# Gated linear attention and an MLP-Mixer on one core: held loads, crossbar transposes and reordered token mixing

## The chip, the cores and the metric

The kernel runs on one core of one Trainium2 chip. The metric is the device time of one execution, in microseconds (us). Most executions of a kernel agree to within a few tenths of a per cent up to about one per cent. An execution that takes over 1.5% longer than the fastest one of the same kernel is called slow and is left out of the comparisons; those that remain are called fast.

Five engines matter here. TensorE (PE in the profile, PEld for its weight loads) does the matrix products. VectorE (DVE) and ScalarE (ACT) do elementwise work and empty PSUM, the memory that TensorE writes its products to. GpSimd (POOL) issues most loads, and SyncE (SP) issues the rest of the DMA transfers. In this kernel every engine works through its own queue in the order of the program, so an instruction that waits also holds up what stands behind it.

## The reference

There are two stages: a gated linear attention whose state is updated token by token, and an MLP-Mixer on its result. B=4, H=8, S=768, D=48; the mixer sees x of shape 4 x 768 x 384.

```python
f = 1.0 / (1.0 + np.exp(-f_logit))
for t in range(S):
    state = f[:, :, t, :, None] * state + np.einsum('bhd,bhe->bhde', k[:, :, t], v[:, :, t])
    y[:, :, t] = np.einsum('bhd,bhde->bhe', q[:, :, t], state)
# ... x = y with the heads side by side: 4 x 768 x 384
h = np.maximum(x.transpose(0, 2, 1) @ w_tok1, 0.0) @ w_tok2     # token mixing, d_tok = 256
u = x + h.transpose(0, 2, 1)
h2 = np.maximum(u @ w_ch1, 0.0) @ w_ch2                         # channel mixing, d_ch = 1536
return u + h2
```

## The kernel before

The attention is done in chunks of 128 tokens, six to a batch, in this way:

- **Gates.** ScalarE turns the forget logits into logarithms of f. They are split into a bf16 high part `Lhi` and a low part `Llo`; the low part is a subtraction.
- **Decayed q and k.** A product with a triangular matrix sums the logarithms over the chunk. Their exponentials `G` and `Gi` scale q and k to `qh` and `kh`.
- **Turning.** `qh` and `kh` have tokens on the partitions. For the scores they are needed with the head dimension there, so TensorE multiplies them by an identity, four products for the eight heads, and ScalarE or VectorE copies the result out of PSUM to `qT` and `kT`.
- **Scores, mask, readout.** The scores are masked (`Am`), and the readout adds the part inside the chunk to the part that comes from the state. The state is copied to a block-diagonal bf16 tile, `state_bd`, for this.

The mixer follows for each batch: token mixing (`tok1`, relu, `tok2`), the sum u, its bf16 copy, three transposing products for each 128 tokens, and the two channel products (`ch1`, `ch2`). In the profile `w_ch_68` is the weight of the first channel product, `w_ch_69` that of the second, and `w_tok_67` that of the second token-mixing product.

```python
if b == 0:                                    # forget logits of batch 0, on SyncE's queue
    for c in range(NCH):
        n = add({"SP": 0.05}, lambda e, c=c: nc.sync.dma_start(out=f_sb[i][:, :, c, :], in_=src[:, :, c, :]),
                key, [])
        made["f", b, c] = add({"Q": 1.1}, None, key + 0.06 * c, [n])
# ... gates: the low half
o = add({"POOL": 0.85 * n, "DVE": 0.4 * n + 0.08} if b > 1 else {"DVE": 0.4 * n + 0.08},
        lambda e: on(e).tensor_tensor(lo, fb, hi, ALU.subtract), key, [g, h])
# ... attention, chunk c of batch b; j = c % 2, p2 = the chunk two before
def turn(name, src, n):
    def fn(e):
        t[name] = p = bank("att", name)
        a = blk(src)
        for hp in range(HP):
            nc.tensor.matmul(p[:, hp * 128:(hp + 1) * 128], lhsT=a[:, hp, :], rhs=ident,
                             start=True, stop=True)
    return fn
tq = made["Tq", b, c] = add({"PE": 0.25}, turn("pq", qh[j], 0), key, [qh_, made.get(("y", *p2))], bank="att")
tk = made["Tk", b, c] = add({"PE": 0.25}, turn("pk", kh[j], 0), key, [kh_, made.get(("A", *p2))], bank="att")
flat = {"ACT": 0.5, "DVE": 0.6}
cq = add(flat, lambda e: copy(e, qT[j], t["pq"].rearrange("p (a t) -> p a t", a=4)),
         key, [made.get(("y", *p2))], frees=tq)
# ... the same for kT
def diag(e):
    copy(e, state_bd[j][0:D, :, 0:D], state[j][0:D])
    copy(e, state_bd[j][64:64 + D, :, D:2 * D], state[j][64:64 + D])
made["bd", b, c] = add({"DVE": 0.5, "ACT": 0.55}, diag, key + 0.02, [s_, made.get(("y", *p2))])
# ... the readout takes state_bd[1 - j], so the one of chunk c - 1
# ... mixing: u, turned on TensorE
def utr(e, tt=tt, t=t):
    t["p"] = bank("mix", "pm")
    for m in range(3):
        nc.tensor.matmul(t["p"][:, m * 128:(m + 1) * 128], lhsT=u_bf[:, tt, m * 128:(m + 1) * 128],
                         rhs=ident, start=True, stop=True)
```

**How the order comes about.** The kernel describes every operation to a planner with `add`: the engines that may do it with an estimated cost for each, the operations that it needs, and a `key`. A small key means early. The planner simulates the engines greedily and emits the instructions in the resulting order; a second number, `at`, gives an earliest time in this simulation. An edit in one place can change the order of instructions everywhere. And the plan chooses the engine of each copy afresh, so two kernels rarely differ in one thing alone.

## Time and profile before

The kernel before takes 204.12 us, the median of three timed runs (203.06 to 204.7). The profiled execution took 202.69 us, so it lies at the fast end of the kernel's runs. Its span, from first to last instruction on the engines, is 200.9 us.

| stretch, us | what goes on | TensorE idle |
|---|---|---|
| 0 to 47 | attention of batch 0, token mixing of batch 0 | about 2 to 7 of each 10 us |
| 50 to 198 | channel products, and attention of the next batch between them | 3.4 in all |

The last figure is 148 us less the 144.56 us for which TensorE was busy in this stretch.

The first fence is from the page of the kernel before. The busy line gives each engine's busy time, its share of the span and its number of instructions (after the x). Each digit of the rows below it is the busy share, in tenths, of one fortieth of the span; in the row PEclk it is the clock that TensorE was granted, in tenths of full speed (9 is 90% or more).

```profile
span 200.9 us, 4497 instructions
...
PE 176.1 (88%) x1768; PEld 110.1 (55%) x1768; DVE 139.7 (70%) x306; ACT 135.1 (67%) x300; POOL 77.8 (39%) x89
...
PE   0547588749999999999999999998999999899993
...
DVE  4459999797998858999999746789546635700222
...
PEclk9999999996999999999999999999999999999999
DMA  8999999999999999999900012010000121100132
```

The row of PE shows two regimes: the holes are in the first tenth to quarter, and after that TensorE is nearly always busy. In the second regime only less TensorE work can make the kernel faster. In the first, only a shorter chain of waits can. The DMA engines are saturated until the middle of the span and nearly idle afterwards.

The table of busy time by stretch shows the same for the start of the kernel before. Columns: the stretch, its length, the busy time of each engine with its number of instructions, the granted TensorE clock, the DMA share and the rate in GB/s.

```profile
core 0: us, PE busy (x) PEld busy (x) DVE busy (x) ACT busy (x) POOL busy (x), PEclk, DMA share, GB/s
...
10.00:20.00 10.00, 6.16 (x77) 4.35 (x77) 7.74 (x18) 6.21 (x17) 8.99 (x11) 1.00 2.57 137
20.00:30.00 10.00, 6.98 (x91) 4.64 (x89) 9.39 (x20) 6.71 (x18) 9.04 (x10) 1.00 1.38 191
...
40.00:50.00 10.00, 7.30 (x76) 4.47 (x76) 8.90 (x21) 8.84 (x19) 9.98 (x12) 0.83 2.27 130
```

From 20 to 30 us VectorE is busy for 9.39 of 10 us.

What a transpose costs TensorE is read from its timeline in a dense stretch of the kernel before. Columns: start, duration, engine, line of the program, operation, output and inputs, shapes, and the number of instructions put together (after the x).

```profile
133.18 0.33 PE L424 MATMUL pm<-ident,u_bf 128*128 128x128 bf16 x3
133.34 0.49 PE L409 MATMUL pm<-h1T,w_tok_67 128*128 128x384 bf16 x2
133.67 0.39 PE L299 MATMUL pq<-ident,qh_86 128*128 128x128 bf16 x4
133.89 0.39 PE L299 MATMUL pk<-ident,kh_88 128*128 128x128 bf16 x4
134.12 1.56 PE L409 MATMUL pm<-h1T,w_tok_67 128*128 128x384 bf16 x6
```

The matmuls are pipelined, so durations overlap and the starts must be used. A group of four for q starts at 133.67 and the next group at 133.89: it holds TensorE 0.22 to 0.23 us. A group of three for u holds it 133.34 - 133.18 = 0.16 us, about 0.17 on the mean of several.

The last fence of before is VectorE's timeline near the start. The bracket gives the idle time before the instruction and what ended it.

```profile
11.93 0.36 DVE L288 TENSOR_TENSOR qh_87<-q_sb_70,G_83 128x384 bf16<-128x384 bf16 x1 [0.97 <-ACT Lhi_78 L250]
...
13.70 0.36 DVE L291 TENSOR_TENSOR kh_89<-k_sb_72,Gi_85 128x384 bf16<-128x384 bf16 x1 [0.64 <-DMA k_sb_72<-in_k_dram]
```

The second chunk's `qh` starts at 11.93 us after a wait of 0.97 us that is put down to a ScalarE instruction for another tile, and `kh` at 13.70 after 0.64 us for its load. ScalarE wrote `G_83`, which this product reads, at 8.50 us for 0.47 us. So `G_83` was there 3 us before.

### The profile page before, as it was taken

The numbers are of one execution on the slowest core, as the hardware profiler recorded it, in microseconds if no ns is written. First come the engines' busy times: TensorE is split into PE (matmuls) and PEld (weight loads), VectorE is DVE, ScalarE is ACT, GpSimd is POOL, SyncE is SP. The second block draws the span as 40 slices with busy tenths as digits, with TensorE's granted clock in tenths as the row PEclk, the third lists the DMA queues.
The fourth block names the chain that finished last, engine by engine and source line by source line (L and its number), as shares of the span: only waits on it lengthen the run. The fifth ranks groups of instructions, "written<-read, shape, count | busy, mean of one in ns | idle before, by whom it ended". The sixth has DMA issues, their size and how long they took to land.

```text
span 200.9 us, 4497 instructions
## 1 busy us (share of the span) xinstructions
PE 176.1 (88%) x1768; PEld 110.1 (55%) x1768; DVE 139.7 (70%) x306; ACT 135.1 (67%) x300; POOL 77.8 (39%) x89
## 2 busy tenths in 40 slices
PE   0547588749999999999999999998999999899993
PEld 0335355335666566666656666656566665456661
DVE  4459999797998858999999746789546635700222
ACT  5857664797988749789999714688897122699000
POOL 7989971299851899739532000000000000000000
PEclk9999999996999999999999999999999999999999
DMA  8999999999999999999900012010000121100132
GB/s 108 170 140 133 159 222 204 167 137 126 194 198 158 122 121 225 203 160 176 118 1 3 0 62 98 3 44 36 3 0 3 39 89 67 42 2 0 39 121 78
DMA packets 88517, 19.95 MB, mean 99 GB/s; under 512 B 81616, under 2 KB 87296, under 8 KB 88496
## 3 DMA queue, kind: packets, MB, share of 16 engines
q0 software_dynamic: 78800, 13.77, 88.4%
q1 hardware_dynamic: 9696, 5.90, 10.7%
q8 instruction: 14, 0.23, 0.5%
q14 instruction: 7, 0.06, 0.1%
HBM read 25.17 MB, written 4.72 MB: 149 GB/s over the span
## 4 chain that ended last, share of the span: by engine, by line
PE 36%; DMA 29%; POOL 14%; DVE 12%; issue 4%; ACT 4%; POOLq 0%; DVEq 0%
PE pm L458 16%; PE pm L439 12%; DMA w_ch_68<-in_moe_w_ch_dram 8%; DMA f_sb_76<-in_f_logit_dram 8%; DMA q_sb_71<-in_q_dram 4%; DMA k_sb_72<-in_k_dram 4%; DMA v_sb_75<-in_v_dram 3%; DVE zT L196 3%; DMA v_sb_74<-in_v_dram 2%; POOL f_sb_77 L225 2%; POOL k_sb_73 L234 2%; POOL q_sb_70 L234 2%; PE pm L390 2%; POOL k_sb_72 L234 2%; POOL v_sb_74 L234 2%
## 5 line engine op out<-in xcount | busy, mean ns | idle before, releaser
L439 PE MATMUL pm<-uT,w_ch_68 128*128 128x384 bf16 x288 | 53.7, 329 | 1.1 <-ACT zT L194 0.6
L458 PE MATMUL pm<-w_ch_69,zT 128*128 128x384 bf16 x288 | 51.6, 326 | 0.1
L194 ACT ACTIVATE zT<-pm 128x384 bf16<-128x384 f32 x80 | 38.4, 497 | 4.5 <-PE pm L439 3.8
L439 PEld LDWEIGHTS <-w_ch_68 128*128 128x128 bf16 x288 | 26.6, 98 | 18.5 <-issue 2.9
L458 PEld LDWEIGHTS <-zT 128*128 128x128 bf16 x288 | 26.9, 98 | 16.4 <-issue 0.2
L234 POOL DMA_DIRECT2D k_sb_73<-in_k_dram x12 | 11.2, 935 | 7.4 <-DMA w_ch_68<-in_moe_w_ch_dram 4.4
L234 POOL DMA_DIRECT2D q_sb_71<-in_q_dram x12 | 11.2, 935 | 4.8 <-DMA f_sb_77<-in_f_logit_dram 4.7
L234 POOL DMA_DIRECT2D k_sb_72<-in_k_dram x12 | 10.9, 907 | 4.8 <-DMA f_sb_76<-in_f_logit_dram 4.8
L234 POOL DMA_DIRECT2D q_sb_70<-in_q_dram x12 | 11.0, 916 | 4.2 <-DMA w_ch_69<-in_moe_w_ch_dram 2.4
L234 POOL DMA_DIRECT2D v_sb_75<-in_v_dram x12 | 11.1, 926 | 1.5 <-PE pA_1448 L315 1.5
L409 PE MATMUL pm<-h1T,w_tok_67 128*128 128x384 bf16 x48 | 11.0, 332 | 0.5 <-ACT h1T L194 0.4
L234 POOL DMA_DIRECT2D v_sb_74<-in_v_dram x12 | 10.8, 904 | 0.6 <-PE pq L299 0.3
L467 DVE TENSOR_TENSOR out_sb_114<-u_nat_110,pm 128x384 f32<-128x384 f32 x2 | 1.1, 554 | 14.0 <-PE pm L458 14.0
L188 ACT CAST x_bf_106<-py 128x384 bf16<-128x384 f32 x7 | 3.3, 477 | 10.6 <-PE py L359 9.5
L424 PE MATMUL pm<-ident,u_bf 128*128 128x128 bf16 x72 | 7.6, 219 | 2.5 <-DVE u_nat_109 L413 0.9
L196 DVE TENSOR_SCALAR zT<-pm 128x384 bf16<-128x384 f32 x16 | 8.6, 550 | 1.4 <-PE pm L439 1.4
L190 DVE COPY x_nat_105<-py 128x384 f32<-128x384 f32 x10 | 5.6, 557 | 5.8 <-ACT x_bf_107 L188 5.8
L188 ACT CAST x_bf_107<-py 128x384 bf16<-128x384 f32 x11 | 5.3, 481 | 6.0 <-PE py L359 5.5
L188 ACT CAST qT_91<-pq 128x512 bf16<-128x512 f32 x11 | 6.6, 596 | 3.9 <-PE pq L299 3.7
L266 PE MATMUL pS<-Lhi_78,tri_bf 128*128 128x384 bf16 x12 | 4.8, 400 | 4.8 <-POOL ident masks.py:197 4.8
L254 DVE TENSOR_TENSOR Llo_80<-f_sb_76,Lhi_78 128x384 bf16<-128x384 f32 (+1 forms) x9 | 6.1, 687 | 3.1 <-ACT f_sb_76 L252 3.1
L424 PEld LDWEIGHTS <-u_bf 128*128 128x128 bf16 x72 | 5.0, 97 | 5.2 <-issue 2.1
(235 smaller groups left out, 421.6 us busy)
## 6 DMA issues: line engine op xcount, KB each, us to landing
f_sb_77<-in_f_logit_dram POOLq DMA_DIRECT2D x2, 1152.0 KB, 12.0
f_sb_76<-in_f_logit_dram SPq DMA_DIRECT2D x6, 192.0 KB, 5.6
q_sb_70<-in_q_dram POOLq DMA_DIRECT2D x12, 96.0 KB, 6.4
k_sb_72<-in_k_dram POOLq DMA_DIRECT2D x12, 96.0 KB, 5.9
v_sb_74<-in_v_dram POOLq DMA_DIRECT2D x12, 96.0 KB, 6.3
w_ch_68<-in_moe_w_ch_dram POOLq DMA_DIRECT2D x1, 1152.0 KB, 15.7
q_sb_71<-in_q_dram POOLq DMA_DIRECT2D x12, 96.0 KB, 10.3
k_sb_73<-in_k_dram POOLq DMA_DIRECT2D x12, 96.0 KB, 6.3
```

Source lines behind the costliest of these rows:

```text
L188: nc.scalar.copy(dst, src)
L190: on(e).tensor_copy(dst, src)
L194: nc.scalar.activation(dst, src, AF.Relu, bias=0.0, scale=1.0)
L196: nc.vector.tensor_scalar(dst, src, 0.0, None, ALU.max)
L225: m = swdge(lambda e: nc.gpsimd.dma_start(out=f_sb[i], in_=src), key, 2.28, 5.9, 0.3, [made.get(("lo", b - 2, c)) for c in range(NCH)], at)
L234: lambda e, dst=dst, src=src: nc.gpsimd.dma_start(out=dst[i][:, c], in_=chunk_of(src, b, c)),
L254: lambda e: on(e).tensor_tensor(lo, fb, hi, ALU.subtract), key, [g, h])
L266: nc.tensor.matmul(Sv, lhsT=tri_bf, rhs=Lhi[i][:, c, :, 0:D], start=True, stop=False)
L409: nc.tensor.matmul(t["p"][:, 0:DM], lhsT=w_tok2[:, kt, tt * 128:(tt + 1) * 128], rhs=h1T[:, kt, :], start=(kt == 0), stop=(kt == 1))
L424: nc.tensor.matmul(t["p"][:, m * 128:(m + 1) * 128], lhsT=u_bf[:, tt, m * 128:(m + 1) * 128], rhs=ident, start=True, stop=True)
L439: nc.tensor.matmul(t["p"][:, 0:384], lhsT=w_ch1[:, kt, cc * 128:(cc + 1) * 128], rhs=uT[:, kt, th * 384:(th + 1) * 384], start=(kt == 0), ...
L458: nc.tensor.matmul(t["p"][:, 0:DM], lhsT=zT[:, kt, tt * 128:(tt + 1) * 128], rhs=w_ch2[:, kt, :], start=(kt == 0), stop=(kt == NCC - 1))
```

## The change

The change has six parts:

1. **Held loads.** In batch 0 the forget logits of chunks 3 to 5 are not loaded at once. Each load has to follow a one-element VectorE memset into its target, which VectorE reaches in its queue only some microseconds later. The intent is that q, k and v of the first chunks need not share the DMA engines with logits that are wanted much later.
2. **Crossbar transposes.** From the 17th chunk on (chunk 4 of batch 2), q and k are turned by a transposing DMA on SyncE's queue (called a crossbar transpose here), and u from batch 2 on. TensorE and the PSUM copies have nothing more to do with these.
3. **Gate subtractions** may go to GpSimd in all batches.
4. **State copies** go to ScalarE in batch 0. The copy now waits for the readout of the chunk before (`p1`), not two before (`p2`), and the state update waits for copies of the state buffer that it overwrites.
5. **FIRST = 0.3**: token mixing gets earlier keys, so that the planner puts it ahead of the next batch's gates.
6. **LEAD and PACE**: the next batch's attention comes slightly earlier.

```diff
         if b == 0:
             for c in range(NCH):
+                held = [] if c < 3 else [add({"DVE": 0.07}, lambda e, c=c: nc.vector.memset(
+                    f_sb[i][0:1, 0, c, 0:1], 0.0), key + 0.06 * c, [], at=1.9 * c - 0.2)]
                 n = add({"SP": 0.05}, lambda e, c=c: nc.sync.dma_start(out=f_sb[i][:, :, c, :], in_=src[:, :, c, :]),
-                        key, [])
+                        key + 0.06 * c, held)
# ...
+    def crossbar(dst, src, key, deps):
+        n = add({"SP": 1.2}, lambda e: nc.sync.dma_start_transpose(out=dst, in_=src), key, deps)
+        return add({"Q": 0.7}, None, key, [n])
# ... gates
-        o = add({"POOL": 0.85 * n, "DVE": 0.4 * n + 0.08} if b > 1 else {"DVE": 0.4 * n + 0.08},
+        o = add({"POOL": 0.85 * n, "DVE": 0.4 * n + 0.08},
# ... attention: the TensorE form is kept under "if NCH * b + c < XBAR_QK:", and
+        else:
+            cq = made["Tq", b, c] = crossbar(qT[j], qh[j].rearrange("t h dd -> t (h dd)"), key,
+                                             [qh_, made.get(("y", *p2))])
+            ck = made["Tk", b, c] = crossbar(kT[j], kh[j].rearrange("t h dd -> t (h dd)"), key,
+                                             [kh_, made.get(("A", *p2))])
# ... state update and state copy
-                                        [z, made.get(("st", b, c - 1))], frees=d)
+                                        [z, made.get(("st", b, c - 1)), made.get(("bd", *p2)),
+                                         made.get(("bd", b - 1, c + NCH - 4)) if c < 2 else None], frees=d)
-            made["bd", b, c] = add({"DVE": 0.5, "ACT": 0.55}, diag, key + 0.02, [s_, made.get(("y", *p2))])
+            made["bd", b, c] = add({"DVE": 0.5, "ACT": 0.65} if b else {"ACT": 0.65}, diag, key + 0.02, [s_, made.get(("y", *p1))])
# ... mixing: the keys of tok1, its relu, tok2, u and the turn of u
-                n = add({"PE": 0.17 * (k1 - k0)}, tok1, key0,
+                n = add({"PE": 0.17 * (k1 - k0)}, tok1, key0 - FIRST,
-            kk = key(0.5)
+            kk = key(0.5) - FIRST
+            if b >= XBAR_U:
+                made["ut", b, tt] = made["cu", b, tt] = crossbar(
+                    uT[:, :, tt * 128:(tt + 1) * 128], u_bf[:, tt, :], kk,
+                    [ub, made.get(("c1", b - 1, tt // 3))])
+                continue
# ...
-    LEAD = (-0.05, 0.13)
-    PACE = (34.0, 5.0)
+    FIRST = 0.3
+    XBAR_QK = 16
+    XBAR_U = 2
+    LEAD = (-0.05, 0.11)
+    PACE = (33.0, 4.5)
```

More of the change, by code (lines that the diff above doesn't have):

```diff
@@ L260, in attention @@
         p2 = (b, c - 2) if c >= 2 else (b - 1, c + NCH - 2)
+        p1 = (b, c - 1) if c >= 1 else (b - 1, NCH - 1)
         t = {}
@@ L301, in turn @@
             return fn
-        tq = made["Tq", b, c] = add({"PE": 0.25}, turn("pq", qh[j], 0), key, [qh_, made.get(("y", *p2))], bank="att")
-        tk = made["Tk", b, c] = add({"PE": 0.25}, turn("pk", kh[j], 0), key, [kh_, made.get(("A", *p2))], bank="att")
-        flat = {"ACT": 0.5, "DVE": 0.6}
-        cq = add(flat, lambda e: copy(e, qT[j], t["pq"].rearrange("p (a t) -> p a t", a=4)),
-                 key, [made.get(("y", *p2))], frees=tq)
-        ck = add(flat, lambda e: copy(e, kT[j], t["pk"].rearrange("p (a t) -> p a t", a=4)),
-                 key, [made.get(("A", *p2))], frees=tk)
+        if NCH * b + c < XBAR_QK:
+            tq = made["Tq", b, c] = add({"PE": 0.25}, turn("pq", qh[j], 0), key,
+                                        [qh_, made.get(("y", *p2))], bank="att")
+            tk = made["Tk", b, c] = add({"PE": 0.25}, turn("pk", kh[j], 0), key,
+                                        [kh_, made.get(("A", *p2))], bank="att")
+            flat = {"ACT": 0.5, "DVE": 0.6}
+            cq = add(flat, lambda e: copy(e, qT[j], t["pq"].rearrange("p (a t) -> p a t", a=4)),
+                     key, [made.get(("y", *p2))], frees=tq)
+            ck = add(flat, lambda e: copy(e, kT[j], t["pk"].rearrange("p (a t) -> p a t", a=4)),
+                     key, [made.get(("A", *p2))], frees=tk)
+        else:
[3 more added lines that the diff above has]
+                                             [kh_, made.get(("A", *p2))])
         def score(e):
@@ L398, in mixing @@
             h = add({"ACT": 0.39, "DVE": 0.47}, lambda e, rt=rt, t=t: relu(e, h1T[:, rt, :], t["p"][:, 0:DM]),
-                    key0, [last, made.get(("t2", b - 1))], frees=first)
+                    key0 - FIRST, [last, made.get(("t2", b - 1))], frees=first)
             hs.append(h)
```

## The prediction

> **What bounds the kernel now.** The table of busy time by stretch shows two regimes. From 50 to 197 us TensorE is idle for only about 3 us. Before 50 us it is busy 3.2, 6.2, 7.0, 7.9 and 7.3 us of each 10. There the list of waits names a dependency chain: 4.8 us at the start, then VectorE results (masked scores 2.0 us, decayed q 1.8, low half of the gates 1.6). VectorE is at 9.4 and 8.8 of 10 us from 20 to 40 us. The DMA engines are over 90% busy until 100 us, then nearly idle.
>
> **Transposes.** By the instruction lists, 100 of TensorE's 264 transposing matmuls go (16 groups of four for q and k, 12 of three for u), with their 28 PSUM evictions, and become 28 crossbar transposes on SyncE's queue. In dense stretches of the timeline a group of four holds TensorE 0.23 us (start to next start), a group of three 0.17. So 16 x 0.23 + 12 x 0.17 = 5.7 us of TensorE work goes, all after about 100 us, where TensorE is critical: it should come off nearly whole. The evictions (0.48 to 0.68 us each, some 15 us over ACT and VectorE) go too, which helps 130 to 140 us, where TensorE had gaps.
>
> It adds latency. No crossbar transpose is in this trace. The Trainium skill ("VectorE: DVE Perf Modes", "The three transpose paths") gives 1309 ns for 128x128 through the crossbar, 390 ns on TensorE. Outputs from the same queue land in 1.9 to 2.6 us, and six f loads took 6.2 us to issue. My estimate: 3 to 4.5 us from issue to landing, 1.2 us apart. For q and k other TensorE work hides that. In the last batch, only 24 matmuls (3.9 us) of filler follow the last token-mixing product before the first channel product, which needs three u transposes; I expect 1 to 2 us of TensorE idle there.
>
> **Start.** Forget logits of chunks 3 to 5 issue later, so q, k and v of the first chunks land earlier: at most 0.7 us each, by the waits. In batch 0 all state copies go to ACT (about 3 us less VectorE time) and two gate subtractions to GpSimd. Token mixing ahead of the gates: before, ACT did gates from 37.6 to 42 us first, and the first channel product began at 47.1 us, although its weight had landed by 39. I expect the dense phase 2 to 3 us earlier.
>
> **Sum.** 5.7 (transposes) + 2.5 (start) + 0.5 (fewer gaps) - 1.5 (crossbar latency at the end) = 7.2 us off 204.1: 196.9 us. Range 193 to 201. Faster by over 2%: 0.82; within 2%: 0.14; slower: 0.04.
>
> **What would show it.** TensorE: 1668 matmuls, busy about 168 us. First channel-product matmul at 44 to 45 us. ACT plus VectorE busy 10 to 15 us less. Crossbar transposes landing in under 4.5 us. In the last batch under 2 us of TensorE idle between token mixing and dense channel products. The final 23 us (144 matmuls at 0.16 us) unchanged.
>
> **What would make it wrong.** If one crossbar transpose holds SyncE or the DMA engines 2 us or more, that in-order queue, which also carries the outputs, becomes the chain in batches 2 and 3, and several us come back. If early loads wait behind GpSimd's subtractions (1.64 us for two chunks), which stand in the queue that issues them, the start gains nothing. If VectorE, at 98% from 90 to 110 us, sets the pace there, the start's gain is lost by 110 us.

## The result, and the profile after

The changed kernel takes 193.90 us, the median of four runs (193.6 to 195.25). The kernel before takes 204.17 us (203.06 to 204.7) beside it. The ratio is 0.9517, with a 95% interval of 0.9457 to 0.9576. A ratio is the mean time of one kernel's fast runs over the mean of the other's fast runs of the same rounds, so it is not quite the ratio of the medians quoted. The mean granted clock in the two profiles was nearly the same (0.992 before, 0.982 after).

The page of the changed kernel, the same lines as before:

```profile
span 192.0 us, 4351 instructions
...
PE 170.5 (89%) x1668; PEld 105.4 (55%) x1668; DVE 129.5 (67%) x286; ACT 129.4 (67%) x292; POOL 81.0 (42%) x92
...
PE   0787896679999999999999899999998999999992
...
DVE  4578888988899757988998973898673637200222
...
PEclk9999999957999999999999999999999999999999
DMA  8999999999999999999999343344532124310222
```

TensorE has exactly 100 instructions fewer and 5.6 us less busy time. The second to sixth digits of its row are higher or the same, the next two lower. The DMA row now has more work in the second half, and the crossbar transposes run there.

The table of busy time by stretch of the changed kernel, the same stretches:

```profile
10.00:20.00 10.00, 7.75 (x97) 5.30 (x98) 8.15 (x19) 9.69 (x27) 10.00 (x13) 1.00 2.46 146
20.00:30.00 10.00, 8.79 (x109) 5.57 (x109) 8.53 (x20) 7.47 (x19) 9.79 (x10) 1.00 1.51 184
...
40.00:50.00 10.00, 10.00 (x110) 6.32 (x110) 8.21 (x18) 8.33 (x20) 10.00 (x11) 0.74 1.91 100
```

VectorE's timeline of the changed kernel, the same two instructions (they are at other lines of the program):

```profile
9.79 0.35 DVE L296 TENSOR_TENSOR qh_87<-q_sb_70,G_83 128x384 bf16<-128x384 bf16 x1
10.08 0.06 DVE L222 MEMSET f_sb_76<- 1x1 f32 x1
...
11.02 0.36 DVE L299 TENSOR_TENSOR kh_89<-k_sb_72,Gi_85 128x384 bf16<-128x384 bf16 x1 [0.89 <-DMA k_sb_72<-in_k_dram]
```

The second chunk's `qh` is 2.1 us earlier and its `kh` 2.7 us earlier. The memset at 10.08 us is the last of the three that hold back a load.

| milestone, us | before | after |
|---|---|---|
| `kh` of chunk 1, batch 0 | 13.70 | 11.02 |
| first product of channel mixing | 47.12 | 42.60 |
| dense channel products of the last batch | 174.21 | 164.73 |
| end of the span | 200.9 | 192.0 |

The profiles differ by 8.9 us: 4.5 us by the first channel product and 4.4 us after it. The last stretch, from the dense products to the end, takes 26.7 us before and 27.3 after (before, three of the 72 products had already started at 173.41 us).

The PEclk rows show one more thing, which the prediction did not consider. By windows of 0.5 us, the granted clock was 0.50 from about 45.5 to 48.5 us before, and from about 38.5 to 45 us after. The first three channel products of the changed kernel took 1.12 us together, against 0.65 us for three at 46.53 us, when the clock was full again. So part of the 4.5 us at this milestone is lost again: after its first channel product TensorE lost about 1.3 us to the low clock in the changed kernel and 0.8 us in the kernel before, an estimate from these windows. No run here was made to find out what sets the clock.

In the list of instructions that concern the tile `uT` in the changed kernel (duration in ns, minimum, median and maximum, then first and last start), the transposing DMA takes this much of SyncE's queue and lands this soon:

```profile
L246 SPq DMA_TRANSPOSE uT<-u_bf x12: 1177/1206/2017, 121.7 to 165.5; - x12
...
DMA to landing us min/median/max: 2.3/2.3/3.9
```

The list of DMA issues of the changed kernel (number, median us from issue to landing) has the q and k transposes too:

```profile
qT_90<-qh_86 SPq DMA_TRANSPOSE x4, 3.3
kT_92<-kh_88 SPq DMA_TRANSPOSE x4, 2.4
```

The Trainium skill, "VectorE: DVE Perf Modes", section "The three transpose paths", gives 1309 ns for a 128x128 bf16 block through the DMA crossbar. Here the queue was held for a median of 1206 ns by a transpose of 128x384 and of 1192 ns by one of 128x512, and the result landed after 2.3 to 3.3 us. The page's figure is near the time on the queue, which was the same at both sizes here.

TensorE's waits from 43 us to the end in the changed kernel (total us, number, longest) show little left over:

```profile
PE pm L461 <- ACT zT L194: 0.8, 1, 0.8
PE pA_1824 L331 <- DMA kT_92<-kh_88: 0.7, 1, 0.7
...
PE pm L426 <- DVE u_nat_110 L430: 0.4, 1, 0.4
```

Its timeline at the end shows why the latency of the crossbar did not hurt there:

```profile
160.37 0.48 PE L426 MATMUL pm<-h1T,w_tok_67 128*128 128x384 bf16 x2 [0.37 <-DVE u_nat_110 L430]
160.83 4.06 PE L480 MATMUL pm<-w_ch_69,zT 128*128 128x384 bf16 x24
164.73 11.86 PE L461 MATMUL pm<-uT,w_ch_68 128*128 128x384 bf16 x72
176.43 11.86 PE L480 MATMUL pm<-w_ch_69,zT 128*128 128x384 bf16 x72
```

The last token-mixing product starts at 160.37 us, 24 products that were waiting fill the next 3.9 us, and the first channel product on `uT` follows at 164.73 with no wait.

### The profile page after: what moved, and what is told of

It reads as the page before. It is cut to its first block, busy times and chain, and to the rows that moved or that the text cites. A ratio compares the mean times of both kernels' runs of the same rounds, so it can differ in the third digit from the quotient of the medians.

```text
span 192.0 us, 4351 instructions
## 1 busy us (share of the span) xinstructions
PE 170.5 (89%) x1668; PEld 105.4 (55%) x1668; DVE 129.5 (67%) x286; ACT 129.4 (67%) x292; POOL 81.0 (42%) x92
## 4 chain that ended last, share of the span: by engine, by line
PE 53%; DVE 18%; ACT 15%; DMA 6%; issue 4%; POOL 2%; DVEq 0%; POOLq 0%; ACTq 0%
PE pm L480 24%; PE pm L461 14%; DMA kT_92<-kh_88 3%; PE pm L407 3%; DMA k_sb_72<-in_k_dram 3%; PE pm L426 2%; ACT zT L194 2%; DVE u_bf L190 2%; PE py L371 1%; ACT state_bd_103 L188 1%; DVE Am_96 L337 1%; DVE Am_95 L337 1%; DVE u_nat_109 L430 1%; ACT u_bf L188 1%; ACT state_bd_102 L188 1%
## 5 line engine op out<-in xcount | busy, mean ns | idle before, releaser
L461 PE MATMUL pm<-uT,w_ch_68 128*128 128x384 bf16 x288 | 54.5, 330 | 1.1 <-ACT zT L194 0.8
L480 PE MATMUL pm<-w_ch_69,zT 128*128 128x384 bf16 x288 | 50.5, 326 | 0.0
L194 ACT ACTIVATE zT<-pm 128x384 bf16<-128x384 f32 x73 | 34.7, 500 | 6.2 <-PE pm L461 5.8
L480 PEld LDWEIGHTS <-zT 128*128 128x128 bf16 x288 | 27.3, 98 | 17.7 <-issue 0.4
L196 DVE TENSOR_SCALAR zT<-pm 128x384 bf16<-128x384 f32 x23 | 12.2, 551 | 1.2 <-PE pm L461 1.2
L237 POOL DMA_DIRECT2D v_sb_75<-in_v_dram x12 | 11.3, 941 | 0.0
L237 POOL DMA_DIRECT2D v_sb_74<-in_v_dram x12 | 11.1, 926 | 0.4 <-issue 0.4
L261 POOL TENSOR_TENSOR Llo_81<-f_sb_77,Lhi_79 128x768 bf16<-128x768 f32 x3 | 5.0, 1669 | 14.7 <-ACT f_sb_77 L259 14.7
L489 DVE TENSOR_TENSOR out_sb_114<-u_nat_110,pm 128x384 f32<-128x384 f32 x2 | 1.1, 550 | 14.1 <-PE pm L480 14.1
L190 DVE COPY x_nat_105<-py 128x384 f32<-128x384 f32 x8 | 4.5, 558 | 6.5 <-ACT x_bf_107 L188 6.4
L190 DVE COPY x_nat_104<-py 128x384 f32<-128x384 f32 x9 | 5.0, 558 | 5.4 <-ACT x_bf_106 L188 5.4
L287 ACT ACTIVATE G_82<-pS 128x384 bf16<-128x384 f32 x12 | 5.9, 488 | 4.2 <-PE pS L281 4.1
L430 DVE TENSOR_TENSOR u_nat_109<-x_nat_104,pm 128x384 f32<-128x384 f32 x12 | 6.2, 550 | 3.6 <-PE pm L426 3.5
## 6 DMA issues: line engine op xcount, KB each, us to landing
f_sb_76<-in_f_logit_dram SPq DMA_DIRECT2D x6, 192.0 KB, 4.5
```

Of the source, the lines that this page charges most:

```text
L190: on(e).tensor_copy(dst, src)
L194: nc.scalar.activation(dst, src, AF.Relu, bias=0.0, scale=1.0)
L196: nc.vector.tensor_scalar(dst, src, 0.0, None, ALU.max)
L237: lambda e, dst=dst, src=src: nc.gpsimd.dma_start(out=dst[i][:, c], in_=chunk_of(src, b, c)),
L287: return lambda e: nc.scalar.activation(dst.rearrange("t h d -> t (h d)"), t["pS"][:, 0:DM], AF.Exp, bias=0.0, scale=scale)
L430: u = made["u", b, tt] = add({"DVE": 0.47}, lambda e, tt=tt, t=t: nc.vector.tensor_tensor(u_nat[i][:, tt, :], x_nat[i][:, tt, :], t["p"][: ...
```

## The experiments

The theories that were to be told apart, in words:

- **TensorE's time.** The gain after the start comes from the 100 transposing matmuls that left TensorE. The rival is the **PSUM copies**: what helped is that ScalarE and VectorE have 28 copies fewer.
- For the start: **VectorE relief** (state copies to ScalarE, subtractions to GpSimd), or **DMA** (held loads let the first q, k and v land earlier), or **order** (token mixing ahead of the gates).

Unless said otherwise an experiment is an edit of the changed kernel. Runs of the kernel before stand beside each: 204.27, 204.32 and 203.96 us in the three groups of runs. The granted clock of the profiled fast runs was between 0.953 and 0.991. Every edit but one re-plans the whole kernel, and I read differences under about 1 us as not resolved. Every kernel whose result was wrong is marked so; all others were correct.

### All transposes back on TensorE

```diff
-    XBAR_QK = 16
-    XBAR_U = 2
+    XBAR_QK = 99
+    XBAR_U = 99
```

> The changed kernel with all transposes on TensorE again (no crossbar); everything else of the change stays. If the crossbar is worth the TensorE work that it takes away (5.7 us less about 1 us of new gaps), the time rises by 4 to 5.5 us to 198 to 199.5 us, with the first channel product still at 42.6 us. If the crossbar's worth lies also in the evictions that ACT and VectorE no longer do, it rises by more than 6 us. If most of the 10 us came from the start and the new order, it rises by less than 3 us.

Measured: 199.95 us, ratio to before 0.9807 (0.9767 to 0.9848). This is 6.05 us slower than the changed kernel. TensorE is at 1768 matmuls and 177.4 us again. The first channel product starts at 42.80 us, as in the changed kernel (42.60), so all of the loss is after the start. The crossbar, in its surroundings, is worth about 6 us. Which resource it relieves is not yet shown, because 28 PSUM copies came back too: ScalarE and VectorE are busy for 271.0 us together, and 258.9 in the changed kernel.

### Idle transposing matmuls put back

The crossbar stays. The 100 matmuls are put back beside it, into PSUM banks that nobody reads.

```diff
                                              [kh_, made.get(("A", *p2))])
+            add({"PE": 0.25}, turn("pq", qh[j], 0), key, [qh_], bank="att")
+            add({"PE": 0.25}, turn("pk", kh[j], 0), key, [kh_], bank="att")
# ... and the three of u in the same way, into a bank "mix"
```

> The changed kernel, crossbar transposes kept, plus the 100 transposing matmuls put back on TensorE at their old places in the order, into a PSUM bank that nobody reads: the TensorE work of the old way without its evictions. u1_all_on_tensor (both back) took 6 us more than the changed kernel. If the gain of the crossbar is TensorE's time, this run gets back to 198.5 to 200 us (5 to 6 us more than 193.9). If it was the evictions that ACT and VectorE no longer do, it stays below 196 us.

Measured: 199.61 us, 0.9761 (0.9723 to 0.98), which is 5.7 us slower than the changed kernel. The busy line of its page:

```profile
PE 177.3 (89%) x1768; PEld 111.5 (56%) x1768; DVE 129.3 (65%) x288; ACT 127.3 (64%) x289; POOL 82.7 (42%) x93
```

VectorE and ScalarE are about where the changed kernel has them (129.5 and 129.4), and nearly the whole loss of 6.05 us is back. TensorE's busy time is 6.8 us above the changed kernel's, and the rest of its span is 0.7 us shorter. So it is TensorE's time, not the copies. The sum that I had made from the timeline, 16 x 0.23 + 12 x 0.17 = 5.7 us, is what was measured, within what a re-plan moves.

### Token mixing not ahead of the gates

```diff
-    FIRST = 0.3
+    FIRST = 0.0
```

> The changed kernel with token mixing given its old place in the order (no head start over the gates of the next batch). If that head start is what brought the first channel product forward, it goes back to 45 to 47 us and the time rises by 2 to 4 us. If the start was won before token mixing begins (the last chunk of batch 0 ready at 31.6 us in place of 36), the first channel product moves by less than 1.5 us and the time by less than 1.5 us.

Measured: 198.48 us, 0.9734 (0.9681 to 0.9787), so 4.6 us slower. But the first channel product starts at 42.34 us, no later than in the changed kernel. In this pair of kernels the order of token mixing and gates does nothing for the start. The loss is later. TensorE's waits from 43 us on begin with this line:

```profile
PE pm L461 <- DMA uT<-u_bf: 4.8, 2, 2.8
```

TensorE twice stands idle for a crossbar transpose of u: 2.8 us before the products at 133.28 us, and 2.1 us before those at 168.22 us, in the last batch. In the changed kernel this wait does not appear. The head start of token mixing is what hides the latency of the crossbar. TensorE's timeline shows the two places:

```profile
133.28 5.74 PE L461 MATMUL pm<-uT,w_ch 128*128 128x384 bf16 x24 [2.76 <-DMA uT<-u_bf]
...
168.22 13.55 PE L461 MATMUL pm<-uT,w_ch 128*128 128x384 bf16 x72 [2.06 <-DMA uT<-u_bf]
```

The waits are not all that each place costs. The 24 products after the first take 5.74 us, where 24 of the same shape take 4.06 in the changed kernel (at 160.83 us), and the 72 after the second take 13.55 us, where the changed kernel needs 11.86. By windows of 0.5 us the granted clock was 0.50 from about 134 to 137 and from about 168 to 171.5 us. Waits and low clock together come to 8.2 us, more than the 4.6 us lost, so some was regained elsewhere: the last channel product of batch 1 starts 1.2 us earlier here (127.9 against 129.1 us).

### Neither crossbar nor head start

```diff
-    FIRST = 0.3
-    XBAR_QK = 16
-    XBAR_U = 2
+    FIRST = 0.0
+    XBAR_QK = 99
+    XBAR_U = 99
```

> The changed kernel without crossbar and without the head start of token mixing: the fourth corner beside 193.9 (both), 198.5 (crossbar alone) and 199.95 (head start alone). If the head start is worth its 4.6 us because it hides the crossbar's latency, it is worth next to nothing here: 199 to 200.5 us. If it helps by itself, this run takes 203 to 205 us. TensorE waits for no transpose DMA in either case, and the waits of the last batch stay under 1 us.

Measured: 199.36 us, 0.974 (0.9692 to 0.9789). With it, four kernels form a square:

| us | FIRST = 0.3 | FIRST = 0 |
|---|---|---|
| with crossbar | 193.90 | 198.48 |
| without | 199.95 | 199.36 |

The crossbar alone is worth 0.9 us, and the head start alone nothing (0.6 us the other way); neither is resolved. Without the crossbar, the first channel product comes at 44.01 us with FIRST = 0 and at 42.80 with FIRST = 0.3, but the time does not follow it. Together they are worth 5.5 us. They are one change in two halves: one frees TensorE, the other keeps it from waiting for what freed it.

### The loads not held, everything else in the same order

The memsets stay in their places, but write a tile that no load touches. No instruction changes its place, so this experiment has no re-plan in it.

```diff
                 held = [] if c < 3 else [add({"DVE": 0.07}, lambda e, c=c: nc.vector.memset(
-                    f_sb[i][0:1, 0, c, 0:1], 0.0), key + 0.06 * c, [], at=1.9 * c - 0.2)]
+                    scratch[0:1, c:c + 1], 0.0), key + 0.06 * c, [], at=1.9 * c - 0.2)]
```

> The changed kernel with every instruction in the same place; only the three one-element memsets write a scratch tile, so the forget-logit loads of chunks 3 to 5 no longer wait for them. Reference points: first mask product of chunk 0 at 14.6 us before and 11.4 after, first channel product at 47.1 before and 42.6 after, span 200.9 and 192.0. Theory L (the early q, k and v landings made the start faster): the k load of chunk 1 lands 2 to 3 us later than in the changed kernel, the first mask goes back towards 14 us, the first channel product to 44.5 to 46 us, and the time rises by 2 to 3 us to 196 to 197 us. Rival V (the 4.2 us less work on VectorE made the start faster, the loads gave at most 0.7 us as I predicted): first channel product within 1 us of 42.6, time within 1 us of the changed kernel.

Measured: 195.98 us, 0.96 (0.9571 to 0.963), so 2.1 us slower. The first channel product is at 45.15 us. VectorE's timeline near the start:

```profile
11.38 0.36 DVE L296 TENSOR_TENSOR qh<-q_sb,G 128x384 bf16<-128x384 bf16 x1 [1.17 <-DMA q_sb<-in_q_dram]
...
13.27 0.36 DVE L299 TENSOR_TENSOR kh<-k_sb,Gi 128x384 bf16<-128x384 bf16 x1 [1.53 <-DMA k_sb<-in_k_dram]
```

These are the two instructions of the earlier fences, nearly back where they were in the kernel before (11.93 and 13.70). Here the wait is named as what it is: the loads of q and k of chunk 1. In the kernel before, the same wait of `qh_87` was put down to ScalarE, whose product for it had been ready for 3 us. The two instructions are 1.6 and 2.2 us later than in the changed kernel (9.79 and 11.02), where I had read "at most 0.7 us each" off the waits. The held loads are worth 2.1 us of the total.

### The held loads alone, on the kernel before

```diff
         if b == 0:
             for c in range(NCH):
+                held = [] if c < 3 else [add({"DVE": 0.07}, lambda e, c=c: nc.vector.memset(
+                    f_sb[i][0:1, 0, c, 0:1], 0.0), key - 1.0, [], at=1.9 * c - 0.2)]
# ...
-                        key, [])
+                        key + 0.06 * c, held)
```

> The kernel before with one addition: the forget-logit loads of chunks 3 to 5 of batch 0 wait for the three one-element memsets, which the order puts early on VectorE (the last near 10 us). No crossbar, no head start, old split, old dependencies, old pace. If the early q, k and v are worth by themselves what they were worth inside the changed kernel (2.1 us), the time is 201.5 to 202.5 us against 204.2, and the first mask product starts near 12 us in place of 14.6. If they only pay together with the other changes of the start, it stays within 0.8 us of before.

Measured: 201.28 us (200.08 to 202.68) beside 203.96 for the kernel before, 0.9871 (0.9797 to 0.9944). It is 2.7 us faster, and the first channel product moves from 47.12 to 44.8 us. From both sides the held loads come to 2 to 3 us.

### State copies and subtractions back on the old engines

```diff
-        o = add({"POOL": 0.85 * n, "DVE": 0.4 * n + 0.08},
+        o = add({"POOL": 0.85 * n, "DVE": 0.4 * n + 0.08} if b > 1 else {"DVE": 0.4 * n + 0.08},
# ...
-            made["bd", b, c] = add({"DVE": 0.5, "ACT": 0.65} if b else {"ACT": 0.65}, diag, key + 0.02, [s_, made.get(("y", *p1))])
+            made["bd", b, c] = add({"DVE": 0.5, "ACT": 0.65}, diag, key + 0.02, [s_, made.get(("y", *p1))])
```

> The changed kernel, but state copies of batch 0 may go to VectorE again, and gate subtractions of batches 0 and 1 go only to VectorE, as before. The loads stay held back. Rival V: VectorE's work before token mixing rises by 3 to 4 us, the first channel product moves from 42.6 to 45.5 to 47 us, the time rises by 3 to 4 us. Theory L: first channel product at most 1.5 us later, time up by at most 1.5 us.

Measured: 200.08 us, 0.9814 (0.9776 to 0.9852). It is 6.2 us slower, with the first channel product at 47.55 us. On its face this confirms VectorE relief. But two lines of its timelines, the first of VectorE and the second of ScalarE, show something else:

```profile
16.77 0.06 DVE L222 MEMSET f_sb<- 1x1 f32 x1
...
22.75 0.52 ACT L255 ACTIVATE f_sb<-f_sb 128x384 f32<-128x384 f32 x1 [0.97 <-DMA f_sb<-in_f_logit_dram]
```

The re-plan put the last of the three memsets behind other VectorE work, at 16.77 us where the changed kernel has it at 10.08. The load that it holds was issued only then, and the gate of the last chunk began at 22.75 us, after a wait for it; in the changed kernel the gates of the last two chunks begin together at 17.66 us. So two things had changed at once.

### The same, with the memsets kept early

The same edit, and the memsets get a key that puts them first in the queue once their planned time has come.

```diff
-                    f_sb[i][0:1, 0, c, 0:1], 0.0), key + 0.06 * c, [], at=1.9 * c - 0.2)]
+                    f_sb[i][0:1, 0, c, 0:1], 0.0), key - 1.0, [], at=1.9 * c - 0.2)]
# ... and the two lines of the experiment before
```

> s_old_split again, but the order now puts the third memset early on VectorE, so that the forget logits of chunk 5 are issued near 10 us as in the changed kernel (in s_old_split they were issued at 16.8 us and the gates of chunk 5 waited). What is left is the old split of state copies and gate subtractions. Rival V (VectorE's work in batch 0 counts): first channel product 3 to 4 us later than 42.6 and time 197 to 198 us. Theory L (only the loads count): at most 1.5 us later, 194 to 195.5 us.

Measured: 194.72 us, the median of three fast runs (193.15 to 195.01; a fourth, of 197.51, was slow at a granted clock of 0.939), and 0.9503 (0.9444 to 0.9561). This is the time of the changed kernel. The last memset is now at 9.84 us. The VectorE relief that this edit takes back is worth nothing that these runs can resolve. It is not all of it: the planner put two of the five state copies of batch 0 back on VectorE (1.3 us, where the kernel before has 3.15) and two subtractions (1.1 us). Of the 5.4 us between this run and the one before, 3.0 had been lost by the first channel product (47.55 against 44.56), which fits the late load. The rest came later, where the run before also waited 1.8 us for a transpose of u and 2.3 us for `zT`; this part may be the re-plan and was not separated. The first channel product is about 2 us later than in the changed kernel, at the same total. So this milestone tells the total only to about 2 us. The clock is one reason: in this run it was 0.50 from about 34 to 40.5 us and full when the channel products began, while in the changed kernel they began at half clock.

### Subtractions of batch 1 not on GpSimd

A look at the changed kernel's trace had shown that two VectorE copies of the same size take very different times while GpSimd does a subtraction. The first two lines are VectorE's, the third is GpSimd's, from the timelines of the changed kernel:

```profile
36.22 0.35 DVE L190 CAST u_bf<-u_nat_109 128x384 bf16<-128x384 f32 x1
...
38.00 1.74 DVE L190 CAST u_bf<-u_nat_109 128x384 bf16<-128x384 f32 x1
...
37.89 3.34 POOL L261 TENSOR_TENSOR Llo_81<-f_sb_77,Lhi_79 128x768 bf16<-128x768 f32 x2 [8.10 <-ACT f_sb_77 L259]
```

```diff
-        o = add({"POOL": 0.85 * n, "DVE": 0.4 * n + 0.08},
+        o = add({"POOL": 0.85 * n, "DVE": 0.4 * n + 0.08} if b != 1 else {"DVE": 0.4 * n + 0.08},
```

> The changed kernel, but the gate subtractions of batch 1 stay on VectorE (those of batches 0, 2 and 3 may go to GpSimd). In the changed kernel two of them hold GpSimd from 37.9 to 41.2 us; a VectorE copy of u that starts at 38.0 then takes 1.74 us where the others take 0.35, TensorE waits 1.2 us for it, and the loads of batch 1 are issued 3 us later. If that is a cost, the copies go back to about 0.35 us, the first channel product comes 1 us earlier and the time is 192 to 193.5 us. If VectorE's extra 1.9 us of subtraction weighs as much, the time is 193.5 to 195 us.

Measured: 194.72 us, 0.9532 (0.9496 to 0.9569), the same as the changed kernel within its interval. VectorE's timeline has the copy back at its short duration:

```profile
38.10 0.36 DVE L190 CAST u_bf<-u_nat 128x384 bf16<-128x384 f32 x1
```

The first channel product came at 42.46 us, so not 1 us earlier. The slowdown is real and goes away with the cause: 1.74 us beside GpSimd's subtraction, 0.36 without. But VectorE then does the subtraction itself, at 0.96 us for two chunks, and the total does not move. The Trainium skill, "Advanced Engine Details and Errata", section "GPSIMD Details", says that GpSimd shares a read and a write interface with VectorE. The trace agrees: this copy took five times as long. It ended at 39.74 us, some 0.2 us after the second of the two subtractions had started (39.5 us), so it may have waited for the first one rather than run slowly. The copies of `uT` out of PSUM next to it kept their 0.55 us.

### Old dependencies and old split

```diff
# ... the early memsets, the old rule for the subtractions, and
-                                        [z, made.get(("st", b, c - 1)), made.get(("bd", *p2)),
-                                         made.get(("bd", b - 1, c + NCH - 4)) if c < 2 else None], frees=d)
+                                        [z, made.get(("st", b, c - 1))], frees=d)
# ...
-            made["bd", b, c] = add({"DVE": 0.5, "ACT": 0.65} if b else {"ACT": 0.65}, diag, key + 0.02, [s_, made.get(("y", *p1))])
+            made["bd", b, c] = add({"DVE": 0.5, "ACT": 0.65}, diag, key + 0.02, [s_, made.get(("y", *p2))])
```

> The changed kernel with everything of the start put back except the held loads: old split of state copies and gate subtractions, and the old dependencies between state copies and readouts that the order is planned with (s_old_split_pinned kept the new ones and took 194.9 us). Crossbar, head start and new pace stay. If the remaining 2 us of the start's gain come from the corrected dependencies, the time is 196 to 197.5 us. If they come from the new pace and lead or the head start, it stays at 194 to 195.5 us.

Measured: 192.84 us, 0.9453 (0.9408 to 0.9498), **and a wrong result**, with a relative error of 0.0433. Its time is not that of a valid kernel and is not used. The order of its instructions shows why. The state copy of chunk 3 in batch 3 is emitted before the readout of chunk 2, which still needs the same `state_bd` buffer. The old dependency named the readout of the chunk two before, which reads the other buffer. In the trace the copy runs at 135.20 us and the readout at 138.16. Nothing reports a race, because the program itself has the two in this order. The kernel before has the same dependency and is correct, so its plan must have put the two the right way round. Part of this change is therefore a repair, and what it costs or brings cannot be measured by undoing it.

### The crossbar from chunk 12 on

```diff
-    XBAR_QK = 16
+    XBAR_QK = 12
```

> The changed kernel with the crossbar also for q and k of chunks 12 to 15 (batch 2 from its first chunk): 8 more groups of four matmuls leave TensorE, 8 x 0.23 = 1.8 us. These transposes fall into 85 to 105 us, where the DMA engines are still over 90% busy with loads; the first k transpose of the changed kernel, issued there at 101 us, took 6.3 us to land where the others take 2.4. If the order hides that, the time is 192 to 193 us and this kernel beats both. If the landing times of 5 us and more show, TensorE waits 2 us or more for transpose DMAs before 105 us and the time is 194 to 196 us.

Measured: 203.98, 204.97, 205.0 and 199.37 us, correct. The first three count as slow beside the last, so there is one fast run and no interval. Even that one is 5.5 us slower than the changed kernel. TensorE has 32 matmuls less than the changed kernel, and it did not help. The profile fell in a slow run and is not used to size anything: in it TensorE waited 4.1 us in one piece for a transpose of k that was under way while the loads of the next batch were running, and the transposes of q took 9.2 us to land at worst, where the changed kernel's worst is 6.3.

### The crossbar from the second batch on

```diff
-    XBAR_QK = 16
-    XBAR_U = 2
+    XBAR_QK = 6
+    XBAR_U = 1
```

> The changed kernel with the crossbar from batch 1 on (q and k from chunk 6, u from batch 1): 20 more groups of four and 6 of three leave TensorE, 20 x 0.23 + 6 x 0.17 = 5.6 us. All of these transposes run between 40 and 105 us, beside loads that keep the DMA engines over 90% busy. If TensorE's time is all that counts, the time is 188 to 189.5 us. If the crossbar pays only after the loads are done, transposes land in 5 us and more, TensorE's waits for transpose DMAs reach several us, and the time is 195 us or more.

Measured: 225.35, 224.53, 223.48 and 220.15 us, correct; the last is the one fast run. It is 26 us slower than the changed kernel and 16 us slower than before, with 198 matmuls fewer than before. Its granted clock was lower too (0.906 in the fast run, 0.963 to 0.988 in the changed kernel), and how much of the 26 us goes with that is not known. The list of the tile `kT`, again from a slow run, points to a mechanism but does not size it:

```profile
L246 SPq DMA_TRANSPOSE kT<-kh x18: 1189/1205/4819, 45.0 to 176.4; - x18
...
  DVE kh L299: 11.1, 4
...
DMA to landing us min/median/max: 2.4/4.2/12.5
```

The line in the middle is from the part on who waited: VectorE waited 11.1 us over four instructions before it could write the next `kh`, because the transpose had not yet read the last one. The Trainium skill, "Advanced Engine Details and Errata", section "X-Bar Transpose (TRN2)", says that transposing DMAs are as fast as ordinary ones. After the loads have ended this agrees, in landing time: in the changed kernel, from 107 us on, transposes land in 2.4 us in the median and outputs of the same queue in 2.0 (an output is 192 KB, a transpose 96 or 128 KB), though a transpose holds the queue for some 1.2 us and an output for 0.33 to 0.43. Beside loads both are slower, and the transposes more so: two transposes before 103 us took 5.9 and 6.3 us, outputs in the same stretch 3.9. Here, in the slow run, it was 7.3 against 4.6, and one transpose landed after 12.5 us. The two limits in the change, 16 and 2, sit at the place where the loads end (about 106 us: 22 of the 40 digits in the DMA row of the changed kernel).

No experiment gave a valid kernel that beats the changed one. The two that come near, both at 194.72 us, are not told apart from it.

## Why the prediction was right or wrong

The prediction was 196.9 us (193 to 201), faster with a chance of 0.82. The result is 193.90 us: faster, inside the range, and 3 us better than the middle.

The gain of 10.3 us by the medians comes apart as follows. Crossbar and head start together are 5.5 to 6.05 us. Some 4.2 to 4.8 us are left. Of these the held loads are 2.1 us when undone in the same order, and 2.7 us when done alone. The split between engines is nothing that shows, as far as it was taken back. Some 1.5 to 2.7 us stay **open**: they may be the new pace and lead, the corrected dependencies, or the luck of the plan. The pace was not tried by itself, and the dependencies cannot be.

- **Transposes, 5.7 us: right.** The count (1668 matmuls) was exact, and two experiments gave 5.7 and 6.05 us. That the matmuls and not the copies matter was predicted in effect, since only TensorE's time entered the sum, and the idle matmuls show it. TensorE's busy time was predicted at 168 us and is 170.5; the 176.1 of the kernel before less the predicted 5.7 would have been 170.4.
- **Latency at the end, -1.5 us: wrong in size.** It was about nothing: 0.37 us of TensorE idle where I expected 1 to 2. The mechanism exists, with 4.8 us of waits where the head start is taken away. I did not see that the head start of token mixing belongs to the crossbar. I read it as a way to begin the dense phase earlier, and for that it did nothing (42.34 us without it, 42.60 with it).
- **Start, +2.5 us: the step that failed, in size and in reasons.** The first channel product came at 42.60 us, not at 44 to 45. I named three reasons. The loads, "at most 0.7 us each", are worth 2.1 to 2.7 us. The order of token mixing is worth nothing that shows here, nor is the relief of VectorE, as far as it was taken back. I had taken the waits as the profile named them, and a wait that names one releaser hides another: `qh_87` was said to wait for ScalarE and waited for its load of q.
- **Fewer gaps, +0.5 us: not tested by itself.** The idle matmuls, which bring back only TensorE work, already account for 5.7 of the 6.05 us, so what is left for the copies is not resolved. ScalarE and VectorE together have 15.9 us less busy time, against 10 to 15 predicted.
- **Landing in under 4.5 us: right in the middle, not at the edge.** The medians are 2.3 to 3.3 us. The worst was 6.3 us, the transpose of k at 101 us, while loads were still running.
- **The final 144 products unchanged: right.** They run from 164.73 to 188.3 us, twice 11.86 us less the overlap.
- **What would make it wrong.** That a slow crossbar makes SyncE's queue the chain did not happen in the changed kernel. With the crossbar starting earlier 5.5 to 26 us come back, by one fast run each. The long waits for transposes in the two slow profiles fit this risk, and part of the added transposes ran beside loads, but these runs do not show that the queue was the chain. The other two risks, late loads behind GpSimd and VectorE's pace at 90 to 110 us, did not cost the gain: it was 4.5 us at the first channel product and 8.9 at the end.

## What to carry to other kernels

Before taking transposes off a saturated TensorE, multiply the start-to-start time of a group by the number of groups: that is the gain, provided that the latency of the other path is covered by work issued earlier; give the producer the head start in the same step, and start where the DMA queues are quiet, for in this kernel both earlier starts were slower. When a product waits for several inputs, check for each input when it was really there, because the profile names only one. If a load is held back by an instruction in another engine's queue, pin that instruction, for it moves with every re-plan.

## What the Trainium skill lacked or had wrong

- "Advanced Engine Details and Errata", section "X-Bar Transpose (TRN2)": transposing DMAs "as fast as regular DMAs" held, in landing time, only after the loads had ended (2.4 us against 2.0 for outputs). Beside loads two transposes of the changed kernel took 5.9 and 6.3 us, and outputs of the same queue 3.9. No page gives the landing time of a transpose beside loads.
- "VectorE: DVE Perf Modes", section "The three transpose paths": the crossbar's 1309 ns is for one 128x128 block. It lacks that a transpose held the queue for about 1.2 us at 128x384 (1206 ns) as at 128x512 (1192 ns). Its 390 ns for TensorE is for a single block; in a dense stream a group of four held TensorE 0.22 to 0.23 us here.
- "DMA: Bandwidth & Descriptors", section "Rules for kernel authors": "A transpose next to ordinary DMAs needs nothing" is about correct results, and these were correct here even where transposes ran beside loads. It lacks the cost in time: the kernel with the crossbar from batch 1 on took 220.15 us at best, against 193.90.
